# Larger query packets, a shorter prologue list and a reordered first batch in a retention and MLP kernel

## The chip, the cores and the metric

The kernel runs on one core of a Trainium2 chip. Its engines are TensorE (matmuls, "PE" in the profile; its weight loads are "PEld"), VectorE ("DVE"), ScalarE ("ACT"), GpSimd ("POOL") and SyncE ("SP"), which here only issues DMAs. The metric is device time in microseconds (us), and a kernel's time is the median of its runs. A change counts as faster or slower when its ratio to the kernel before is clear of 1 by more than 2%; a 95% interval stands beside each ratio.

## The reference

There are two stages. The first is a retention layer: attention without softmax, in which each score is weighted by a power of a decay per head. The second mixes tokens through a low-rank pair U, V, adds, and applies an MLP.

```python
# q, k, v: (8 batches, 8 heads, 576 tokens, 64), fp32
scores = (q @ k.T) / sqrt(64)
D[i, j] = gamma[h] ** (i - j) if i >= j else 0
ret = (scores * D) @ v                     # per batch and head
x = ret, heads put side by side            # (8, 576, 512)
u = x + ((x.T @ U) @ V).T                  # U: (576, 32), V: (32, 576)
out = u + relu(u @ w1) @ w2                # w1: (512, 2048), w2: (2048, 512)
```

## The kernel before

Batches are taken in pairs. The 1152 tokens of a pair make nine chunks of 128 rows; chunk XC = 4, the joint chunk, holds the last 64 tokens of the even batch and the first 64 of the odd one. The decay is split into a factor for q and a factor for k and v, so that each chunk needs one triangular mask (`ret`), and a running state k^T v per batch (`ps_s`, copied to `s_sb`) carries the past chunks. The MLP works on nine groups of four chunks of 128 tokens. Its first layer is called Y1 below and its second Y2. TensorE has about 320 us of work, and attention of later batches is woven in between the matmuls of the MLP.

A planner in the kernel simulates the engines and writes down a fixed order of instructions for each. Every engine then runs its list strictly in that order. An instruction that waits holds up everything behind it on its engine, and any edit lets the planner find another order elsewhere.

The loads, and what becomes of them, are the part that the change touches. In the kernel before, each chunk loads q and k as a pair into one staging buffer, and a row of the transfer is one head of one token: 64 values of 4 bytes, or 256 B.

```python
N = dict(kq=5, vs=6, qkv=8, qkT=6, ret=6, s_sb=3, ...)          # buffers of each kind
kqs = [sbuf(f"kq_{i}_st", [P, 2, H, D], FP32) for i in range(N["kq"])]
...
for n, (j, dram) in enumerate(((1, k), (0, q), (2, v))):        # in load(p, c, ...)
    ...
    nc.sync.dma_start(out=f[rw, :, :],
        in_=dram[b, :, t0:t0 + rw.stop - rw.start, :].rearrange("h s d -> s h d"))
...
if early:                                                       # the first pair
    ck = pl.op("ACT", 660.0, lambda e: cast(e, 1, 2), [got[1]], ...)      # k, to bf16
    cq = pl.op("DVE", 700.0, qsc, [got[0], ck, cons], ...)                # q times its factor
    cv = pl.op("POOL", 1050.0, vsc, ..., alt=[("DVE", 700.0)])            # v times its factor
else:                                                           # the other pairs
    ck = cq = pl.op("DVE", 700.0, lambda e: cast(e, 0, 2), [got[1], got[0]], ...)  # k and q
```

V is loaded four times, into four groups of 32 partitions. The loads of the first pair are issued in one fixed line: q and k of the first batch, three of its v, U, the rest of v, V, the weights, then the second batch.

```python
for i in range(4):
    nc.sync.dma_start(out=vst[i * R:(i + 1) * R, :], in_=moe_V)
...
first = [0, 1, XC, 2, 3]
line = [ld[x, (0, c)] for c in first for x in "kq"] + [ld["v", (0, c)] for c in (0, 1, 2)]
line += [ld["lu"], ld["v", (0, XC)], ld["v", (0, 3)], ld["lv"]] + ld["lw"]
line += [ld[x, (0, c)] for c in range(5, NCH) for x in "kq"]
line += [ld["v", (0, c)] for c in range(5, NCH)]
```

## Time and profile before

The median was 346.05 us of three runs (346.04 to 346.5). These are lines of the profile's page.

```profile
span 346.1 us, 5817 instructions
...
PE 323.8 (94%) x2348; PEld 158.8 (46%) x2348; DVE 142.4 (41%) x206; ACT 136.6 (39%) x237; POOL 72.7 (21%) x97
...
PE   2679989999998899999999999999999999999995
...
DMA  9979999999999999999999999951211131011002
GB/s 165 210 155 357 385 273 246 225 239 196 186 221 198 221 203 182 238 200 213 196 193 212 204 206 207 216 138 31 82 59 29 30 91 61 2 61 61 2 36 85
...
PE 71%; DMA 14%; SPq 6%; DVE 4%; issue 1%; ACT 1%; POOL 0%; DVEq 0%; POOLq 0%
```

The second line gives busy time and share of the span for each engine. The next rows cut the span into 40 slices of 8.65 us: busy tenths of TensorE and of the DMA engines, and what the DMAs moved. The last line shares out the chain of work that ended last. TensorE is 94% busy, and short of it at three places: the first three slices, the sixth (43 to 52 us), and the 13th and 14th (104 to 121 us). The DMA row is full up to about 225 us. It moves only some 200 GB/s where q, k and v arrive and 385 GB/s where the weights do (fifth slice).

The view by windows gives sizes to these. The columns are the window, its length, and busy time with number of instructions for TensorE, its weight loads, DVE, ACT and POOL; then the clock, the DMA share and GB/s.

```profile
0.00:30.00 30.00, 18.79 (x189) 11.65 (x189) 14.06 (x35) 15.02 (x28) 7.38 (x19) 1.00 0.99 195
50.00:80.00 30.00, 27.12 (x262) 14.70 (x261) 18.52 (x28) 15.72 (x29) 9.28 (x11) 1.00 1.01 224
100.00:130.00 30.00, 26.86 (x212) 12.89 (x210) 14.43 (x19) 9.03 (x16) 7.18 (x9) 1.00 1.07 212
```

I also use a second measure, "gaps": the time from one matmul's start to the next one's, less 0.213 us for 512 columns and in proportion for fewer (the spacing seen in full stretches is 0.216 us), counted where it exceeds 15 ns. By it the kernel before loses 17.9 us from 0 to 30 us, 6.4 from 50 to 80 and 4.8 from 100 to 130.

Three marks on TensorE's timeline: the first MLP matmul at 31.60 us ("MLP 0"), the first of the second group at 75.69 ("MLP 1"), and the end.

### The profile page before, as it was taken

To read this page: it belongs to the slowest core of one execution; us is meant where nothing else is said; L and a number is where in the kernel's file an instruction comes from. 1 tells how busy PE (TensorE), PEld (TensorE's weight loads), DVE (VectorE), ACT (ScalarE), POOL (GpSimd) and SP (SyncE) were. 2 spreads that over 40 slices of the span, in tenths; PEclk is the share of its full clock that TensorE was granted. 3 is DMA by queue.
4 is the path that set the end of the run, shared out by engine and by line. 5 is a ranking of instruction groups with operands and counts; after the bars stand their busy time and mean duration, and the time that the engine had idled before them with its cause. 6 is when DMAs were issued, how large, how long until landed. Compare 5 with 4: busy or idle time off the path is not lost.

```text
span 346.1 us, 5817 instructions
## 1 busy us (share of the span) xinstructions
PE 323.8 (94%) x2348; PEld 158.8 (46%) x2348; DVE 142.4 (41%) x206; ACT 136.6 (39%) x237; POOL 72.7 (21%) x97
## 2 busy tenths in 40 slices
PE   2679989999998899999999999999999999999995
PEld 1354434545543444454445445544544444444442
DVE  2743106657645452565527436734453020021011
ACT  5535636458720354035512641255115405503600
POOL 1046671232231221312213112310110010011010
PEclk9999999999999999999999999999999999999999
DMA  9979999999999999999999999951211131011002
GB/s 165 210 155 357 385 273 246 225 239 196 186 221 198 221 203 182 238 200 213 196 193 212 204 206 207 216 138 31 82 59 29 30 91 61 2 61 61 2 36 85
DMA packets 159769, 56.39 MB, mean 163 GB/s; under 512 B 153088, under 2 KB 153088, under 8 KB 159744
## 3 DMA queue, kind: packets, MB, share of 16 engines
q1 hardware_dynamic: 157024, 47.12, 70.6%
q0 software_dynamic: 2720, 8.92, 8.0%
q8 instruction: 18, 0.29, 0.4%
q14 instruction: 7, 0.06, 0.1%
HBM read 37.14 MB, written 9.44 MB: 135 GB/s over the span
## 4 chain that ended last, share of the span: by engine, by line
PE 71%; DMA 14%; SPq 6%; DVE 4%; issue 1%; ACT 1%; POOL 0%; DVEq 0%; POOLq 0%
PE ps_big_t L263 61%; DMA kq_st<-in_q_dram 9%; SPq L297 5%; PE ps_o L263 4%; PE ps_s L263 4%; DMA kq_st<-in_k_dram 2%; PE ps_sc L263 2%; DMA v_st<-in_v_dram 2%; DMA ust<-in_moe_U_dram 1%; DVE ret_t L438 1%; DVE qkv_t L318 1%; SPq L578 1%; DVE u_t L566 1%; DVE o_sb L672 1%; DVE qkv_t L322 1%
## 5 line engine op out<-in xcount | busy, mean ns | idle before, releaser
L263 PE MATMUL ps_big_t<-uT_t,w_sb 128*128 128x512 bf16 x576 | 134.0, 379 | 1.0 <-DMA uT_t<-u_t 1.0
L263 PE MATMUL ps_big_t<-w_sb,y_t 128*128 128x512 bf16 x576 | 133.0, 379 | 0.0
L648 ACT ACTIVATE y_t<-ps_big_t 128x512 bf16<-128x512 f32 x144 | 86.0, 597 | 99.1 <-PE ps_big_t L263 98.9
L263 PEld LDWEIGHTS <-w_sb 128*128 128x128 bf16 x576 | 53.8, 98 | 63.8 <-issue 3.4
L263 PEld LDWEIGHTS <-y_t 128*128 128x128 bf16 x576 | 54.0, 98 | 63.1 <-issue 2.9
L672 DVE TENSOR_TENSOR o_sb<-ps_big_t,u_t 128x512 f32<-128x512 f32 x36 | 24.8, 688 | 86.1 <-PE ps_big_t L263 84.4
L322 POOL TENSOR_TENSOR qkv_t<-v_st,vscale 128x512 bf16<-128x512 f32 x32 | 33.5, 1047 | 98.1 <-DMA v_st<-in_v_dram 61.4
L678 POOL DMA_DIRECT2D out_dram<-o_sb x34 | 19.2, 564 | 153.4 <-DVE o_sb L672 153.4
L438 DVE TENSOR_TENSOR ret_t<-ps_sc,tri 128x1024 bf16<-128x1024 f32 (+1 forms) x36 | 39.2, 1099 | 19.6 <-PE ps_sc L263 19.6
L406 ACT ACTIVATE s_sb<-ps_s 128x512 bf16<-128x512 f32 x32 | 19.1, 596 | 64.0 <-PE ps_s L263 64.0
L318 DVE CAST qkv_t<-kq_st 128x1024 bf16<-128x1024 f32 x27 | 20.6, 764 | 27.9 <-DMA kq_st<-in_q_dram 27.9
L502 DVE TENSOR_TENSOR x_t<-ps_o,qscale 128x512 bf16<-128x512 f32 x27 | 18.6, 687 | 13.9 <-PE ps_o L263 13.8
L369 PE MATMUL ps_big_t<-ident,qkv_t 128*128 128x128 bf16 x112 | 12.4, 251 | 10.9 <-ACT qkv_t L316 9.0
L566 DVE TENSOR_TENSOR u_t<-ps_s,x_t 128x512 bf16<-128x512 f32 x20 | 13.7, 687 | 16.5 <-PE ps_s L263 16.5
L263 PEld LDWEIGHTS <-qkT_t 64*128 64x128 bf16 (+1 forms) x544 | 14.6, 98 | 12.2 <-issue 7.9
L376 ACT ACTIVATE qkT_t<-ps_big_t 128x512 bf16<-128x512 bf16 x28 | 16.4, 594 | 6.6 <-PE ps_big_t L369 6.1
L263 PEld LDWEIGHTS <-ret_t 128*128 128x128 bf16 x288 | 13.6, 102 | 9.0 <-DVE ret_t L438 1.6
L263 PE MATMUL ps_sc<-qkT_t 64*128 64x128 bf16 x288 | 15.4, 230 | 1.0 <-DVE ret_t L438 0.8
L263 PE MATMUL ps_o<-qkv_t,ret_t 128*128 128x64 bf16 x288 | 15.3, 199 | 0.8 <-DVE ret_t L438 0.6
L322 DVE TENSOR_TENSOR qkv_t<-kq_st,qscale 128x512 bf16<-128x512 f32 x9 | 6.2, 690 | 22.6 <-DMA kq_st<-in_q_dram 22.6
L369 PEld LDWEIGHTS <-qkv_t 128*128 128x128 bf16 x112 | 7.9, 109 | 15.6 <-ACT qkv_t L316 10.6
L263 PE MATMUL ps_s<-qkv_t 128*128 128x128 bf16 (+1 forms) x128 | 13.3, 230 | 1.0 <-POOL qkv_t L322 0.5
(58 smaller groups left out, 121.8 us busy)
## 6 DMA issues: line engine op xcount, KB each, us to landing
out_dram<-o_sb POOLq DMA_DIRECT2D x34, 256.0 KB, 3.1
kq_st<-in_k_dram SPq DMA_DIRECT2D x32, 256.0 KB, 4.9
kq_st<-in_q_dram SPq DMA_DIRECT2D x32, 256.0 KB, 5.1
v_st<-in_v_dram SPq DMA_DIRECT2D x32, 256.0 KB, 5.2
y_t<-in_moe_w_ch_dram SPq DMA_DIRECT2D x10, 512.0 KB, 8.5
wst_t<-in_moe_w_ch_dram SPq DMA_DIRECT2D x6, 512.0 KB, 6.9
kq_st<-in_k_dram SPq DMA_DIRECT2D x8, 128.0 KB, 4.1
kq_st<-in_q_dram SPq DMA_DIRECT2D x8, 128.0 KB, 4.4
```

The source lines that it names most:

```text
L263: nc.tensor.matmul(*a, skip_group_check=True, **kw)
L297: i = nc.sync.dma_start(out=f[rw, :, :], in_=dram[b, :, t0:t0 + rw.stop - rw.start, :].rearrange("h s d -> s h d"),)
L318: nc.vector.tensor_copy(**args)
L322: eng.tensor_tensor(out=qkv[slot(*qk)][:, j, :, :], in0=f, in1=by[:, c, :, None].to_broadcast([P, H, D]), op=ALU.mult,)
L369: nc.tensor.transpose(pst()[:, hp, :], t[:, j, 2 * hp:2 * hp + 2, :].rearrange("p h d -> p (h d)"), ident,)
L406: nc.scalar.activation(out=s_sb[slot(*sk)], in_=ps_s.rearrange("p (a b) -> p a b", b=P), func=AF.Copy)
L438: nc.vector.tensor_tensor(out=ret[slot(*rk)][:, s], in0=ps_sc[:, s], in1=m[:, None, None, :].to_broadcast([P, n, NHP, P]), op=ALU.mult,)
L502: nc.vector.tensor_tensor(out=xs[slot(*xk)].rearrange("p hp hl d -> p hl hp d"), in0=ps_o[:, :, 0:NHP * D].rearrange("p hl (hp d) -> p hl ...
L566: nc.vector.tensor_tensor(out=us[slot(*uk)].rearrange("p (hp hl d) -> p hp hl d", hl=2, d=D), in0=bank().rearrange("p (hp hl d) -> p hp hl ...
L648: nc.scalar.activation(out=y1s[slot(*yk)][:, f, :], in_=ps_big[slot(*bk)], func=AF.Relu)
L672: nc.vector.tensor_tensor(out=osb[slot(*ok)], in0=ps_big[slot(*bk)], in1=us[slot(*uk)], op=ALU.add)
L678: eng.dma_start(out=out_flat[row:row + P, :], in_=osb[slot(*ok)])
```

## The change

The intent is to shorten the stretch before TensorE is full. It has six parts.

1. The q of batches 0 and 1 comes in one 1 MB DMA each. A partition takes four neighbouring tokens, so a row is 1 KB. The rows are then in the wrong order; the four PSUM evacuations of q^T put it right.
2. The joint chunk is computed in 64x64 blocks instead of whole.
3. Chunks 1 and 3 of the first batch put their scores into two other PSUM buffers, so that they need not wait for the mask of the chunk before.
4. V is loaded once and copied three times on GpSimd; U's second half is loaded after the weights.
5. k, q and v have separate staging buffers (12, and 4 for q), and k and q are cast apart.
6. The planner may look 150 ns ahead on DVE and ACT, and the first batch runs in the order 0, 1, 2, 3, XC.

```diff
+    LOOK = {"DVE": 150.0, "ACT": 150.0}
-    N = dict(kq=5, vs=6, qkv=8, qkT=6, ret=6, s_sb=3, x=7, u=12, wst=6, osb=3)
+    N = dict(st=12, q4s=4, qkv=8, qkT=6, ret=6, s_sb=3, x=7, u=12, wst=6, osb=3)
 ...
+    def load_q4(par, prio):
+            nc.sync.dma_start(
+                out=q4.rearrange("p (h x) -> p h x", h=H),
+                in_=q[par, :, t0:t0 + 4 * P, :].rearrange("h (p r) d -> p h (r d)", r=4))
 ...
+            st["q", c] = pl.op("DVE", 700.0, ..., alt=[("POOL", 1050.0)])      # q times its factor
+    def t_q4(par, prio):
+        pst = ps_sc.bitcast(BF16).rearrange("p a b n -> p (a b n)").rearrange(
+            "p (r hp l) -> p r hp l", r=4, hp=NHP)                             # two PSUM banks
+        for i in range(4):
+                args = dict(
+                    out=qkT[slot("qkT", (0, c))][:, 0:NHP, :].rearrange("p hp (l r) -> p hp l r", r=4),
+                    in_=pst[:, :, :, 32 * i:32 * i + 32].rearrange("p r hp l -> p hp l r"))
+            st["qT", c] = pl.op("ACT", 600.0, ev, pes, ..., rel=[sck], alt=[("DVE", 650.0)])
 ...
-            ck = cq = pl.op("DVE", 700.0, lambda e: cast(e, 0, 2), [got[1], got[0]], prio + 4, [qk])
+            ck = pl.op("DVE", 370.0, lambda e: cast(e, 1), [got[1]], prio + 4, [qk])
+            st["q", c] = pl.op("DVE", 370.0, lambda e: cast(e, 0), [got[0], ck], prio + 4, rel=[home[0]])
 ...
-            for i in range(4):
-                nc.sync.dma_start(out=vst[i * R:(i + 1) * R, :], in_=moe_V)
+            nc.sync.dma_start(out=vst, in_=moe_V)
+            for i in range(1, 4):
+                gp.tensor_copy(out=VV[i * R:(i + 1) * R, 0:S], in_=VV[0:R, 0:S])
 ...
-        for n, c in enumerate((0, 1, XC, 2, 3)):
+        for n, c in enumerate((0, 1, 2, 3, XC)):
-            SC(0, c, pr + 3, with_q=False, split=True)
+            SC(0, c, pr + 3, with_q=False, apart=c in (1, 3))
 ...
-    line = [ld[x, (0, c)] for c in first for x in "kq"] + [ld["v", (0, c)] for c in (0, 1, 2)]
-    line += [ld["lu"], ld["v", (0, XC)], ld["v", (0, 3)], ld["lv"]] + ld["lw"]
-    line += [ld[x, (0, c)] for c in range(5, NCH) for x in "kq"]
+    line = [ld["q4", 0]] + [ld["k", (0, c)] for c in first] + [ld["q", (0, XC)]]
+    line += [ld["lv"], ld["lu"]] + [ld["v", (0, c)] for c in first] + ld["lw"]
+    line += [ld["q4", 1]] + [ld["k", (0, c)] for c in range(5, NCH)] + [ld["lub"]]
```

## The prediction

> **What bounds the kernel now.** By the page's busy row, TensorE: 323.8 of 346.1 us at full clock (0.999). From the first MLP matmul at 31.6 us (timeline) it is nearly full, and no work is taken from it. Lost are (a) the 31.6 us before, with about 18 us of TensorE gaps, (b) about 6.4 us of gaps from 50 to 80 us (second batch's attention under the first MLP group; the largest, 2.0 us at 50.5, waits for that batch's first keys), (c) about 5 us from 100 to 130 us, (d) a 4 us tail. (a) and (b) are DMA-bound: the page's DMA row stands at 9 tenths from 0 to 210 us, and the chain of waits names loads of q, k, v and U before these gaps.
>
> **What the change does.** q, k, v come in 256-byte packets, 1024 for each 256 KB, a load every 1.2 to 1.3 us (10 to 16 us: 5065 packets, 213 GB/s). Weights in 2 KB packets take 87 ns each against 18 to 25 ns for 256 B: 389 GB/s. This agrees with the Trainium skill, "DMA: Bandwidth & Descriptors", Specifications, which puts line rate at transfers of at least 512 B. My estimate from these for 1 KB rows is 45 ns a packet, so 1 MB of q takes 2.8 us in place of about 5: 2.3 us saved in each of batches 0 and 1. U's second half (576 packets of 128 B) moves behind the weights: 0.5 us. V once instead of four times: 0.6 us of bytes; and 5 small issues of 0.4 to 0.6 us leave SyncE's queue between 16 and 23.5 us, where DMA ran at only 149 to 174 GB/s and the first weights landed 4.5 us after the last v (29.1, 24.6).
>
> Added: three VV copies (0.6 to 0.7 us), k casts (1.0) and q scalings (1.05) on GpSimd, in all about 13 us before the weight casts, which fits into its waits for DMA. q's reordering rides on the four PSUM evacuations (0.6 us each). Two score buffers take the mask (1.28 us) off the matmul path, but the prologue waits for DMA, so that is worth little. The joint chunk in 64x64 blocks saves about 0.6 us of DVE in each of four chunks, off the critical path; separate k and q casts cost DVE a little.
>
> **Sum.** The first batch's last v lands near 21 us (24.6), the first MLP matmul comes near 26.5 (31.6): 5 us, all critical. The weights' end moves from 46.5 to about 42. The second batch needs 1 MB of q before its first transposes, so its first stall stays (about 2 us), but its last v comes 1.5 to 2 us sooner still; second MLP group near 67.5 against 75.7: 8 us, of which I give 1 back (one Y2 group moves before it). The later gaps stay, because loads and TensorE move together.
>
> **Prediction: 338.7 us**, 8 in 10 between 334.5 and 343.0. Faster by over 2% (below 339.1): 0.55; within 2%: 0.42; slower: 0.03.
>
> **What would show it.** 1 KB packets near 45 ns; last first-batch v near 21 us; first MLP group from 25.5 to 28 us, second from 66 to 70; TensorE gaps of 4 to 6 us between 45 and 75; TensorE's busy time unchanged within 2 us; from the second MLP group to the end about 270 us, as before.
>
> **What would make it wrong.** GpSimd's longer list delays v's scaling or the first weight casts; 1 KB packets no faster per byte; the 1 MB load delays all transposes; the planner's new look-ahead reorders ACT and DVE so that later gaps grow; four q staging buffers (five before) slow the later prefetch. Upwards: the gaps from 100 to 130 us shrink too.

## More of the kernel before

Between 100 and 130 us TensorE lacks 3.1 us. Two more views say why. First the waits of DVE from 70 to 140 us (us in total, times, longest):

```profile
DVE qkv_t L318 <- DMA kq_st<-in_q_dram: 22.4, 11, 5.1
```

Then DVE's timeline there (start, length, and in brackets the idle time before it and what ended it):

```profile
104.29 0.69 DVE L318 CAST qkv_t<-kq_st 128x1024 bf16<-128x1024 f32 x1 [2.81 <-DMA kq_st<-in_q_dram]
104.90 0.68 DVE L566 TENSOR_TENSOR u_t<-ps_s,x_t 128x512 bf16<-128x512 f32 x1
...
122.86 0.69 DVE L318 CAST qkv_t<-kq_st 128x1024 bf16<-128x1024 f32 x1 [2.67 <-DMA kq_st<-in_q_dram]
123.46 0.68 DVE L502 TENSOR_TENSOR x_t<-ps_o,qscale 128x512 bf16<-128x512 f32 x1
```

And TensorE's:

```profile
105.63 0.38 PE L263 MATMUL ps_s<-a_sb,VV 128*128 128x512 bf16 x1 [1.28 <-DVE u_t L566]
...
116.47 1.89 PE L263 MATMUL ps_big_t<-uT_t,w_sb 128*128 128x512 bf16 x8 [1.04 <-DMA uT_t<-u_t]
...
124.20 0.29 PE L263 MATMUL ps_o<-s_sb,qkT_t 64*128 64x64 bf16 x8 [0.82 <-DVE x_t L502]
```

A cast of q and k waits on DVE for its load. The results that TensorE needs, `u_t` and `x_t`, stand behind it in DVE's list, and TensorE waits for those.

In the first batch the view by tile gives the same picture: DVE waits for all five q loads (6.3 us) and ACT for all five k loads (4.4 us). Busy time hides some of what TensorE loses, because a matmul of 128 columns counts 0.31 us in the first 22 us and 0.22 us after 30 us.

## The result

The changed kernel took 341.66 us (340.43 to 341.9, four runs), against 346.27 us (346.04 to 347.2, four runs) for the kernel before in the same rounds. The ratio is 0.9855, with a 95% interval of 0.9824 to 0.9885: faster by 1.45%, which is within 2%. Ratios here and below are the mean time of one kernel's fast runs over that of the other's of the same rounds, so they are not quite the ratio of the medians quoted.

The time lies inside the predicted range, 3 us above its middle. A gain of over 2%, to which the prediction gave 0.55, did not come. The terms of the sum did worse, and that is the subject of the rest.

The page of the changed kernel:

```profile
span 339.8 us, 5955 instructions
...
PE 320.3 (94%) x2412; PEld 159.2 (47%) x2412; DVE 156.1 (46%) x227; ACT 132.8 (39%) x234; POOL 86.0 (25%) x116
...
GB/s 212 202 292 390 385 249 262 213 258 211 206 236 197 229 183 223 210 219 207 183 238 224 195 216 202 125 15 44 66 64 15 69 87 31 0 64 62 0 64 63
...
PE 89%; DVE 5%; DMA 2%; issue 1%; ACT 1%; POOL 0%; DVEq 0%; POOLq 0%
```

DMA had 14% of the chain that ended last, and now has 2%; TensorE's share of it rose from 71% to 89%. The weights' rate is reached one slice sooner. The same windows as before:

```profile
0.00:30.00 30.00, 18.10 (x211) 12.55 (x212) 14.31 (x30) 13.46 (x27) 20.70 (x38) 1.00 1.09 258
50.00:80.00 30.00, 27.66 (x290) 16.08 (x290) 25.06 (x35) 15.55 (x30) 10.84 (x14) 1.00 1.09 237
100.00:130.00 30.00, 30.00 (x235) 14.51 (x234) 18.78 (x25) 12.40 (x21) 6.89 (x8) 1.00 1.07 210
```

From 0 to 30 us TensorE is no busier than before, although the DMAs moved a third more (258 GB/s against 195). From 100 to 130 us it is full. The same stages side by side:

| | before | after | predicted |
|---|---|---|---|
| first weight load issued, us | 23.5 | 17.7 | - |
| MLP 0, us | 31.60 | 30.09 | 26.5 (25.5 to 28) |
| MLP 1, us | 75.69 | 72.39 | 67.5 (66 to 70) |
| from MLP 1 to the end, us | 270.4 | 267.4 | about 270 |
| gaps, 50 to 80 us | 6.4 | 4.9 | 4 to 6 from 45 to 75 |
| gaps, 100 to 130 us | 4.8 | 1.2 | "stay" |
| TensorE busy, us | 323.8 | 320.3 | within 2 of before |

The spans differ by 6.3 us and the medians by 4.6. The profiled execution of the kernel before was a slow one for it, 347.9 us on the timer against a median of 346.27; that of the changed kernel was 341.9 against 341.66. Single stages can therefore be off by a microsecond or so. One such place shows: at 50.5 us the kernel before loses 2.0 us to its wait for the second batch's first k, and b_fastq1 (below), which loads the same things up to 60.7 us, loses 0.6 there. So some 1.4 of the 3.3 us at MLP 1 may be the slow execution's. A repeat of the changed kernel, told of below, had MLP 0 at 29.31 us.

### The prologue: loads sooner, first state matmul not

The first batch on DVE, before:

```profile
8.23 0.69 DVE L322 TENSOR_TENSOR qkv_t<-kq_st,qscale 128x512 bf16<-128x512 f32 x1 [2.33 <-DMA kq_st<-in_q_dram]
8.84 1.28 DVE L438 TENSOR_TENSOR ret_t<-ps_sc,tri 128x512 bf16<-128x512 f32 x2
...
24.66 0.69 DVE L322 TENSOR_TENSOR qkv_t<-v_st,vscale 128x512 bf16<-128x512 f32 x1 [2.67 <-DMA v_st<-in_v_dram]
```

And in the changed kernel:

```profile
6.57 2.14 DVE L307 TENSOR_TENSOR qkv_t<-q_st,qs 128x512 bf16<-128x512 f32 x2 [3.74 <-DMA q_st<-in_q_dram]
10.31 0.69 DVE L359 COPY qkT_t<-ps_sc 128x512 bf16<-128x512 bf16 x1 [1.60 <-PE ps_sc L343]
11.67 0.69 DVE L359 COPY qkT_t<-ps_sc 128x512 bf16<-128x512 bf16 x1 [0.66 <-ACT qkT_t L357]
14.29 1.23 DVE L533 TENSOR_TENSOR ret_t<-ps_sc,tri 128x1024 bf16<-128x1024 f32 x1 [1.93 <-PE ps_sc L278]
...
17.75 1.09 DVE L307 TENSOR_TENSOR qkv_t<-st_st,vscale 128x512 bf16<-128x512 f32 x1
```

ACT does the other two of the four evacuations:

```profile
11.04 0.60 ACT L357 ACTIVATE qkT_t<-ps_sc 128x512 bf16<-128x512 bf16 x1 [1.51 <-DVE qkT_t L359]
12.39 0.60 ACT L357 ACTIVATE qkT_t<-ps_sc 128x512 bf16<-128x512 bf16 x1 [0.76 <-DVE qkT_t L359]
```

GpSimd has a list it did not have before (before, it did nothing on this batch until 17.22 us, when the first v landed):

```profile
6.62 2.99 POOL L307 TENSOR_TENSOR qkv_t<-q_st,qs 128x512 bf16<-128x512 f32 x2 [2.47 <-DMA q_st<-in_q_dram]
...
16.24 2.06 POOL L816 COPY VV<-VV 32x576 bf16<-32x576 bf16 x3
18.39 2.36 POOL L307 TENSOR_TENSOR qkv_t<-st_st,vscale 128x512 bf16<-128x512 f32 x2
```

Here is what to see. In the kernel before the first q is on DVE at 5.21 us, the chunks follow each other as their loads land, and the first mask starts at 8.84. In the changed kernel nothing starts before the whole megabyte has landed at 6.5 us; two scalings each on DVE and GpSimd take until 9.6; the four evacuations run strictly in turn, DVE, ACT, DVE, ACT, from 10.31 to 12.99; the first mask starts at 14.29. Then DVE is at masks until 17.8 us without a pause, and GpSimd has V to copy. So the first v, which no longer waits for DMA (no bracket at 17.75 and 18.39), is scaled at 17.75 us against 17.22. It landed at 16.17 us, 0.9 us sooner than before (17.08), and then lay for 1.6 us. The first state matmul, k^T v, needs it, and starts at 18.90 us against 18.60.

From there to MLP 0 comes a serial run: for each chunk a state matmul, its evacuation, the output matmul, its evacuation, a transpose and the product with U. It took 13.0 us before, with waits for v and U in it, and 11.2 us in the change, with no wait for a load. All of the prologue's gain is here.

The missing waits need not be the whole cause of it; I had overlooked TensorE's clock. The same product with U is slow at first and then fast, here in the changed kernel:

```profile
21.82 0.61 PE L278 MATMUL ps_big_t<-x_t,UU 128*32 128x512 bf16 x1
...
24.81 0.39 PE L278 MATMUL ps_big_t<-x_t,UU 128*32 128x512 bf16 x1
```

The trace's first record of a full clock is at 24.73 us. Until then matmuls of 128 columns follow each other every 107 ns, later every 56. In the kernel before, that record is at 28.16 us, and the product still takes 0.61 us at 27.43. (The page prints a clock of 1.00 also where it has no record; in a_onebuf the stretch from 14.0 to 24.3 us is recorded, as 0.5.) Over all 14 traces the run from the first state matmul to MLP 0 is 0.48 us longer for each microsecond of it that lies before the full clock (correlation 0.98). From before to after that part shrank from 9.6 to 5.8 us, which by this line is 1.8 us, as much as the run shrank. So the clock is a rival to the waits as the cause of this gain. No run separates them, and none shows what brings the full clock on.

### From 100 to 130 us: the wait that went away

DVE's waits for loads from 70 to 140 us were 22.4 us before. In the changed kernel the same view has one line of that kind:

```profile
DVE qkv_t L403 <- DMA q_st<-in_q_dram: 0.9, 1, 0.9
```

The loads of the second pair (batches 2 and 3) start at 52.6 us, against 62.6. The tenth chunk after the first pair, which is the first of the third pair, has its k load issued at 91.7 us, against 105.8. MLP 1 moved by 3.3 us in the same time. The view of waits lists none for TensorE between 100 and 130 us.

### The profile page after: what moved, and what is told of

Same layout as the page of the kernel before. It is cut to its first block, busy times and chain, and to the rows that moved or that the text cites. A ratio compares the mean times of both kernels' runs of the same rounds, so it can differ in the third digit from the quotient of the medians.

```text
span 339.8 us, 5955 instructions
## 1 busy us (share of the span) xinstructions
PE 320.3 (94%) x2412; PEld 159.2 (47%) x2412; DVE 156.1 (46%) x227; ACT 132.8 (39%) x234; POOL 86.0 (25%) x116
## 4 chain that ended last, share of the span: by engine, by line
PE 89%; DVE 5%; DMA 2%; issue 1%; ACT 1%; POOL 0%; DVEq 0%; POOLq 0%
PE ps_big_t L278 73%; PE ps_o L278 6%; PE ps_s L278 5%; PE ps_sc L278 4%; DMA q_st<-in_q_dram 2%; DVE ret_t L533 2%; DVE qkv_t L307 1%; PE ps_big_t L452 1%; PE ps_sc L343 1%; DVE qkv_t L403 1%; ACT qkT_t L357 1%; DVE qkT_t L359 1%; POOL qkv_t L307 0%; DVE o_sb L776 0%; DVE u_t L670 0%
## 5 line engine op out<-in xcount | busy, mean ns | idle before, releaser
L776 DVE TENSOR_TENSOR o_sb<-ps_big_t,u_t 128x512 f32<-128x512 f32 x36 | 24.8, 689 | 90.4 <-PE ps_big_t L278 88.1
L307 POOL TENSOR_TENSOR qkv_t<-st_st,vscale 128x512 bf16<-128x512 f32 x32 | 33.9, 1063 | 52.0 <-DMA st_st<-in_v_dram 26.1
L533 DVE TENSOR_TENSOR ret_t<-ps_sc,tri 128x1024 bf16<-128x1024 f32 x30 | 36.6, 1219 | 18.4 <-PE ps_sc L278 18.4
L403 DVE CAST qkv_t<-st_st 128x512 bf16<-128x512 f32 x27 | 21.5, 795 | 0.8 <-DMA st_st<-in_k_dram 0.8
L278 PEld LDWEIGHTS <-qkT_t 64*128 64x128 bf16 (+2 forms) x576 | 15.0, 100 | 13.4 <-issue 7.1
L278 PEld LDWEIGHTS <-ret_t 128*128 128x128 bf16 (+1 forms) x320 | 13.3, 103 | 9.2 <-DVE ret_t L533 1.6
L278 PE MATMUL ps_sc<-qkT_t 64*128 64x128 bf16 (+1 forms) x304 | 13.7, 221 | 4.0 <-ACT qkT_t L459 2.1
L278 PE MATMUL ps_o<-qkv_t,ret_t 128*128 128x64 bf16 (+1 forms) x320 | 15.2, 197 | 0.9 <-DVE x_t L600 0.5
L403 DVE CAST qkv_t<-q_st 128x512 bf16<-128x512 f32 x27 | 14.3, 529 | 1.4 <-DMA q_st<-in_q_dram 1.4
L278 PEld LDWEIGHTS <-qkv_t 128*128 128x128 bf16 (+1 forms) x128 | 9.2, 102 | 6.1 <-issue 2.1
L670 DVE TENSOR_TENSOR u_t<-ps_o,x_t 128x512 bf16<-128x512 f32 x16 | 10.9, 684 | 1.7 <-PE ps_o L278 1.6
```

Source lines behind the costliest of these rows:

```text
L278: nc.tensor.matmul(*a, skip_group_check=True, **kw)
L307: eng.tensor_tensor(out=out, in0=f, in1=by[:, :, None].to_broadcast([P, H, D]), op=ALU.mult)
L403: nc.vector.tensor_copy(**args)
L533: nc.vector.tensor_tensor(out=ret[slot(*rk)][:, hl, :, 0:n], in0=bank(hl.start)[:, None] if apart else ps_sc[:, hl, :, 0:n], in1=m[:, None ...
L670: nc.vector.tensor_tensor(out=us[slot(*uk)].rearrange("p (hp hl d) -> p hp hl d", hl=2, d=D), in0=bank().rearrange("p (hp hl d) -> p hp hl ...
L776: nc.vector.tensor_tensor(out=osb[slot(*ok)], in0=ps_big[slot(*bk)], in1=us[slot(*uk)], op=ALU.add)
```

## The experiments

Twelve runs followed. The names say what each starts from: "a" from the changed kernel, "b" from the kernel before. Each was timed in three to five rounds beside the kernel before, which had medians of 346.21, 347.35 and 346.74 us, and each has one profile. For all runs:

| run | median, us | ratio to before, 95% | MLP 0 | first state matmul | gaps 100 to 130 |
|---|---|---|---|---|---|
| the change | 341.66 | 0.9855 [0.9824, 0.9885] | 30.09 | 18.90 | 1.2 |
| a_again, the change once more | 341.79 | 0.9849 [0.9806, 0.9892] | 29.31 | 18.19 | 2.0* |
| a_banksplit | 341.0 | 0.9849 [0.9809, 0.9889] | 28.96 | 17.24 | 1.2 |
| a_fastv0, wrong | 341.05 | 0.985 [0.9827, 0.9874] | 29.68 | 18.51 | 1.2 |
| a_q256 | 343.62 | 0.9922 [0.9889, 0.9955] | 31.69 | 18.22 | 1.3 |
| a_onebuf | 343.18 | 0.9871 [0.9829, 0.9913] | 30.06 | 18.07 | 2.0* |
| a_nolook | 340.8 | 0.9799 [0.9752, 0.9845] | 29.19 | 18.89 | 2.1* |
| a_xcwhole | 344.42 | 0.9912 [0.9845, 0.998] | 28.49 | 18.32 | 2.0* |
| a_best | 341.12 | 0.9829 [0.9791, 0.9868] | 29.74 | 19.48 | 2.3* |
| b_fastq1, wrong | 343.24 | 0.9909 [0.9881, 0.9937] | 31.44 | 18.49 | 1.3 |
| b_uv | 345.94 | 0.996 [0.9912, 1.0007] | 32.48 | 18.18 | 5.1* |
| b_split | 345.96 | 0.9974 [0.9922, 1.0026] | 30.35 | 18.10 | 4.2* |
| b_uvsplit | 347.03 | 0.9999 [0.995, 1.0047] | 32.20 | 18.27 | 4.7* |

The traces marked * lack some forty matmul records more than the others, and each missing record looks like a gap of 0.22 us or more. By the stretches where nothing waits, that adds about 0.8 us to 30 us, so 2.0 there is about 1.2, and 4.2 about 3.4.

Two questions were put. Why did the prologue give 1.5 us instead of 5? And why did the gaps from 100 to 130 us close, which I had said would stay?

### a_banksplit: evacuations of different banks

Theory: the four evacuations run in turn because all four read both PSUM banks, and this delays the masks and all after them. The edit lays q^T out so that each bank holds two of the four head pairs, and splits each evacuation by bank: ACT reads one, DVE the other. Buffers are taken at the transposes, and the planner counts free buffers when one operation takes two of a pool.

```diff
-            "p (r hp l) -> p r hp l", r=4, hp=NHP)
+            "p (hp r l) -> p r hp l", r=4, hp=NHP)
...
+            for half in range(2):
+                hs = slice(2 * half, 2 * half + 2)
...
+                        out=qkT[slot("qkT", (0, c))][:, hs, :].rearrange("p hp (l r) -> p hp l r", r=4),
+                        in_=pst[:, :, hs, 32 * i:32 * i + 32].rearrange("p r hp l -> p hp l r"))
...
+                st["qT", c].append(pl.op(("ACT", "DVE")[half], 400.0, ev, pes, ..., rel=[sck]))
```

> The change, but q^T leaves PSUM in halves by bank (two head pairs each): ScalarE from one bank, VectorE from the other, at the same time, where the change has the two engines take turns (10.3 to 13.0 us). Theory 'the prologue is a chain of compute': the four copies end near 12 us, the first MLP group starts about 1 us sooner (29.0 to 29.4 us against 30.1), total 0.5 to 1 us below the change. Rival 'the prologue is still bound by DMA': first MLP group unchanged at 30.1, total unchanged.

The evacuations did run side by side. This is DVE's timeline:

```profile
10.13 1.42 DVE L364 COPY qkT_t<-ps_sc 128x256 bf16<-128x256 bf16 x4 [1.60 <-PE ps_sc L343]
12.64 1.22 DVE L539 TENSOR_TENSOR ret_t<-ps_sc,tri 128x1024 bf16<-128x1024 f32 x1 [1.09 <-PE ps_sc L278]
```

They end at 11.55 us instead of 12.99, and the first mask starts 1.65 us sooner. The first state matmul came 1.66 us sooner, at 17.24 (against the repeat of the change, told of below, 1.34 for the mask and 0.95 for the matmul). But the run from there to MLP 0 grew from 11.2 to 11.7 us, and the median fell by 0.7 us, which the intervals don't separate from nothing. So the order of the evacuations is a real cost, but the next limit lies close behind it: the last v had to wait for its load there (0.95 us on GpSimd at 22.56), and the first one had landed at 15.95 us, only 0.16 us before DVE scaled it.

### a_fastv0: is it still the DMA?

The rival says that the prologue still waits for DMA. In this run the first batch's v comes in 2 KB rows of contiguous memory. The values are wrong (relative error 0.52), but every other step is the same.

```diff
+                    if j == 2 and p == 0 and c <= XC:
+                        n = (rw.stop - rw.start) * H * D
+                        a0 = t0 * H * D
+                        sent.append(nc.sync.dma_start(
+                            out=f[rw, :, :].rearrange("p h d -> p (h d)"),
+                            in_=dram[b].rearrange("h s d -> (h s d)")[a0:a0 + n].rearrange("(p x) -> p x", x=H * D),
+                        ))
+                        continue
```

> The change, but the first batch's v (and the joint chunk's) come in 2 KB rows of the same bytes, so with wrong data on purpose: about 4 us less DMA in the prologue. Theory 'chain of compute': first MLP group within 0.5 us of 30.1. Rival 'still bound by DMA': it starts 2 to 4 us sooner. Total: within 1.5 us of the change by the theory, 3 us or more below it by the rival.

The last v was issued at 14.97 us instead of 17.06, and the first weight at 15.6 instead of 17.7: 2.1 us less of DMA, where I had expected 4. The first v landed at 15.61 us instead of 16.17, and DVE scaled it at 17.78, no sooner than in the change (17.75). MLP 0 came at 29.68 us, between the 30.09 and 29.31 of the change's own two traces. The ratio, 0.985, is the change's. The rival falls: two microseconds less of DMA in the prologue buy nothing that can be told from the scatter.

### a_q256: without the 1 KB rows

The q of the first pair is loaded chunk by chunk in 256 B rows again; all else is the change.

```diff
-        wide = p == 0 and c != XC
+        wide = False
...
-        load_q4(0, base - 3.0)
-        t_q4(0, base - 2.0)
...
-    line = [ld["q4", 0]] + [ld["k", (0, c)] for c in first] + [ld["q", (0, XC)]]
+    line = [ld[x, (0, c)] for c in first for x in "kq"]
```

> The change, but q of the first two batches in 256-byte rows again, chunk by chunk, transposed as in the kernel before; V once, staging, casts, look-ahead, two score buffers and 64x64 blocks kept. Theory 'the 1 KB rows pay through the lead of the loads': first MLP group within 1.5 us of 30.1, but the later loads 4 to 5 us later, so second MLP group 74 to 76 us, TensorE gaps from 100 to 130 us back to 2 to 4 us (1.2 with the change), total 343 to 346. Rival 'the order of instructions or VectorE's lighter load closed the gaps': gaps from 100 to 130 stay under 1.5 us.

It took 343.62 us, ratio 0.9922 against 0.9855, so the 1 KB rows with all that hangs on them are worth about 0.7%. The trace shows that this isn't the prologue alone. MLP 0 is at 31.69 us, 1.6 later, but MLP 1 is at 72.20, no later than the change's 72.39, because gaps from 50 to 80 us are 2.7 us in place of 4.9. The change's second batch also waits for a whole megabyte of q and four evacuations in turn. Nor did the gaps from 100 to 130 us come back to 2 to 4 us, as my theory of the 1 KB rows had it: at 1.3 us they kept to what its rival said. What is lost is one stall that the change doesn't have:

```profile
151.17 0.41 PE L278 MATMUL ps_o<-qkv_t,ret_t 128*128 128x64 bf16 x8 [2.67 <-DVE ret_t L533]
```

Behind it DVE waited 1.59 and 1.68 us for two loads, issued at 143.5 us and later, after a DMA transpose had held SyncE's list from 140.7 to 143.5. Whether every run of this kernel has this stall is not known; I have one trace of it.

### b_fastq1: only the loads of the second pair, on the kernel before

Theory: the gaps from 100 to 130 us are waits for loads of the second pair. In this run only that pair's q is loaded in 2 KB rows of contiguous memory (wrong values again, relative error 0.67). Nothing else differs from the kernel before.

```diff
+                    if j == 0 and p == 1:
+                        ...                     # the same 2 KB rows as in a_fastv0, for q
+                        continue
```

> The kernel before, but q of the second pair of batches in 2 KB rows of as many bytes, so with wrong data on purpose: less DMA after 62 us, nothing else touched. Theory 'gaps from 100 to 130 us are VectorE's queue standing behind casts that wait for q': first and second MLP group unchanged (31.6, 75.7), VectorE's waits for q between 70 and 140 us fall from 22 us to under 8, TensorE gaps from 100 to 130 fall from 4.8 us to under 2, total 342 to 344. Rival 'order and VectorE load': gaps stay at 4 us or more, total 346.

Gaps from 100 to 130 us fell from 4.8 to 1.3 us, and DVE's waits for loads from 22.4 to 12.9 us (I had expected under 8). The time fell to 343.24 us, ratio 0.9909. MLP 0 stayed where it was (31.44). This shows that the gaps were load waits. Relief for the loads of the second pair is worth about 0.9% by itself, more than half of what the whole change gained. MLP 1 came 2.2 us sooner, at 73.47, and gaps from 50 to 80 us fell from 6.4 to 4.3 us, which I had not expected; but 1.4 us of that is at 50.5 us, before the first of the changed loads was issued, so the edit did not cause it. From MLP 1 to the end the trace is 3.3 us shorter.

### b_uv: V once and U's second half later, on the kernel before

What in the change closes those gaps? My first theory was that any relief of the DMA early on is enough, since the DMAs are full up to about 225 us. This run has part 4 of the change alone.

```diff
-            for i in range(4):
-                nc.sync.dma_start(out=vst[i * R:(i + 1) * R, :], in_=moe_V)
+            nc.sync.dma_start(out=vst, in_=moe_V)
...
+            for i in range(1, 4):
+                gp.tensor_copy(out=VV[i * R:(i + 1) * R, 0:S], in_=VV[0:R, 0:S])
...
-    line += [ld["lu"], ld["v", (0, XC)], ld["v", (0, 3)], ld["lv"]] + ld["lw"]
-    line += [ld[x, (0, c)] for c in range(5, NCH) for x in "kq"]
+    line += [ld["lv"], ld["lu"], ld["v", (0, XC)], ld["v", (0, 3)]] + ld["lw"]
+    line += [ld[x, (0, c)] for c in range(5, NCH) for x in "kq"] + [ld["lub"]]
```

> The kernel before with one part of the change alone: V loaded once and copied on GpSimd, U's second half behind the second batch's keys. Theory 'a small relief of DMA and of SyncE's queue gives most of the lead': the first weight load is issued near 20.5 us (23.5 before, 17.7 with the change), the first MLP group starts at 30 to 31 us (31.6), TensorE gaps from 100 to 130 us fall from 4.8 to under 2.5, total 342 to 344. Rival 'the 1 KB rows are needed for it': gaps from 100 to 130 stay at 4 us or more and the total at 345 to 346.

The weights were issued 4.1 us sooner (19.4), yet MLP 0 came 0.9 us later, at 32.48: the casts and copies of V and U take GpSimd from 20.3 to 24.4 us, DVE scales the v's at 22.98 and 24.16 us, the first of them after 2.82 us of waiting for its load, and TensorE waits 1.64 us at 24.30 for a result that stands behind it on DVE. DVE's waits barely changed:

```profile
DVE qkv_t L318 <- DMA kq_st<-in_q_dram: 21.0, 10, 5.4
```

The gaps stayed (5.1), and the time is 345.94 us, ratio 0.996 with an interval that holds 1. The theory falls. MLP 1 came 2.6 us sooner and the k load of the tenth chunk after the first pair 2.7 us sooner: here loads and TensorE moved together, as the prediction had said.

### a_onebuf: one score buffer in the first batch

```diff
-            SC(0, c, pr + 3, with_q=False, apart=c in (1, 3))
+            SC(0, c, pr + 3, with_q=False, apart=False)
```

> The change, but all score blocks of the first batch in the one buffer, masks whole, as elsewhere. Theory 'the prologue is a chain of compute': first MLP group 0.5 to 1.5 us later than 30.1, total up by as much. Rival, as I predicted ('worth little, the prologue waits for DMA'): within 0.3 us.

MLP 0 is at 30.06 us, which is the change's 30.09. The median is 343.18 us, 1.4 to 1.5 above the change's, but the ratio (0.9871 against 0.9855) is not separated from it. The first state matmul came no later. The second buffers are worth little in the prologue, as predicted.

### a_nolook: the planner without its look-ahead

```diff
-    LOOK = {"DVE": 150.0, "ACT": 150.0}
+    LOOK = {}
```

> The change without the planner's look-ahead on VectorE and ScalarE, so another order of a few instructions. Theory 'the gain is the lead of the loads': total within 1 us of the change, gaps from 100 to 130 us under 2. Rival 'the new order closed the gaps': they come back to 4 us, total 344 or more.

It took 340.8 us, ratio 0.9799: nothing is lost without the look-ahead, and nominally 0.9 us is gained (1.9 us by the ratios, as the kernel before was slower). The gaps from 100 to 130 us stay closed. This run also gives a measure of luck. It computes the same things in another order, and differs from the change by 1 to 2 us. No part that is worth less than that can be told from the planner's rearrangement.

### a_xcwhole: the joint chunk whole

```diff
-        n = HALF if c == XC else P
+        n = P
...
+        cols = slice(0, HALF) if c == XC else slice(0, P)
```

> The change, but the joint chunk whole again (128x128 scores, block mask, full state copy). VectorE's mask for it takes 1.2 us again in place of 0.69 in each of four chunks. Theory: off the critical path, total within 0.7 us of the change, gaps from 100 to 130 us under 2. Rival 'VectorE's lighter load closed the gaps': they come back to 3 us or more, total 343 or more.

It took 344.42 us (342.28 to 347.4), ratio 0.9912 with the wide interval 0.9845 to 0.998. That is nominally 0.6% worse than the change, although MLP 0 came at 28.49 us, the earliest of all. The trace is that of the slowest run, with a stall of 2.4 us at 147.6 us, and a clock recorded at 0.5 from 151.4 to 158.2 us; no other trace has such a stretch after 30 us and before its end. The mean granted clock doesn't order the runs: the fastest had 0.983, and two of 344.4 us had 0.998 and 1.0. The blocks may be worth up to 2 us, or the order may have been unlucky. This stays open.

### b_split: separate staging and casts, on the kernel before

My second theory for the gaps: the joint cast of k and q waits for both loads at the head of DVE's list, and the change casts them apart, from buffers that are freed one by one. This run has part 5 alone, with 16 staging buffers.

```diff
-    N = dict(kq=5, vs=6, qkv=8, qkT=6, ret=6, s_sb=3, x=7, u=12, wst=6, osb=3)
+    N = dict(st=16, qkv=8, qkT=6, ret=6, s_sb=3, x=7, u=12, wst=6, osb=3)
...
-            ck = cq = pl.op("DVE", 700.0, lambda e: cast(e, 0, 2), [got[1], got[0]], prio + 4, [qk])
+            ck = pl.op("DVE", 370.0, lambda e: cast(e, 1), [got[1]], prio + 4, [qk])
+            cq = pl.op("DVE", 370.0, lambda e: cast(e, 0), [got[0], ck], prio + 4)
```

> The kernel before with another part of the change alone: one staging buffer for each load (16) in place of 5 pairs and 6, and k and q cast apart on VectorE; loads, V and all else as before. Theory 'a cast that waits for both loads of a pair holds up VectorE's queue': first and second MLP group unchanged (31.6, 75.7), VectorE's waits for loads between 70 and 140 us fall from 22 us to under 12, TensorE gaps from 100 to 130 us from 4.8 to under 2.5, total 342 to 344. Rival 'it takes less DMA': gaps stay at 4 us or more, total 345.5 to 347.

The gaps stayed for the most part (4.2, or about 3.4 with the missing records allowed for), and DVE waited 17.8 us for loads. The time is 345.96 us, ratio 0.9974. The second theory falls as well.

### b_uvsplit: both parts together

The edit is that of b_uv and that of b_split, in one kernel.

> The kernel before with both: V once and U's second half later, and one staging buffer for each load with k and q cast apart; q still in 256-byte rows. Theory 'neither alone, both together': total 342.5 to 344.5, gaps from 100 to 130 us under 2.5, near the change with q in 256-byte rows (343.6). Theory 'the 1 KB rows are needed': 345 or more, gaps at 4 us or more.

The time is 347.03 us, ratio 0.9999, with gaps of 4.7 us. Parts 4 and 5 together don't close the gaps.

### a_again: the change once more

No edit; it is a measure of the scatter, in five rounds.

> The changed kernel once more, unchanged, as the measure for the next run on the same chip: 341 to 342.5 us.

It took 341.79 us (341.48 to 341.87). Its MLP 0 was at 29.31 us, 0.8 us before that of the first trace, and 0.7 of that was there at the first state matmul already. Single marks of one trace are good to about 0.8 us; the medians agree within 0.15 us.

### a_best: a version meant to beat both

This joins what the runs suggested: evacuations split by bank as in a_banksplit, q scaled on DVE alone, and v on GpSimd alone.

```diff
+            ...                                  # evacuations and buffer count as in a_banksplit
-                [got, ld["consts"]], prio + 0.1, acq=[("qkv", (0, c))], rel=[keys[r]],
-                alt=[("POOL", 1050.0)])
+                [got, ld["consts"]], prio + 0.1, acq=[("qkv", (0, c))], rel=[keys[r]])
...
-            cv = pl.op("POOL", 1050.0, vsc, [got[2], ck, cons], prio + 1.2, alt=[("DVE", 700.0)])
-            if c == NCH - 1:
-                cv.engs = [("DVE", 700.0)]
+            cv = pl.op("POOL", 1050.0, vsc, [got[2], ck, cons], prio + 1.2)
```

> The change, with q^T's halves leaving PSUM at the same time by bank, and in the first two batches q scaled on VectorE alone and v on GpSimd alone, so that neither stands behind the other[...] (1.53 us in place of 0.69 for VectorE, 1.54 in place of 1.04 for GpSimd). Theory 'the prologue is a chain of compute with those two waits in it': first MLP group 28.3 to 29.3 us (30.1), gaps from 50 to 80 us under 4 (4.9), total 1 to 2.5 us below the change. Rival: first MLP group as with the banks alone (29.0), total within 0.7 us of the change.

DVE's timeline shows that the first half of the plan worked:

```profile
6.40 2.50 DVE L307 TENSOR_TENSOR qkv_t<-q_st,qs 128x512 bf16<-128x512 f32 x4 [3.58 <-DMA q_st<-in_q_dram]
9.68 1.42 DVE L363 COPY qkT_t<-ps_sc 128x256 bf16<-128x256 bf16 x4 [0.78 <-PE ps_sc L342]
12.18 1.23 DVE L536 TENSOR_TENSOR ret_t<-ps_sc,tri 128x1024 bf16<-128x1024 f32 x1 [1.09 <-PE ps_sc L278]
```

GpSimd's shows where the gain went:

```profile
16.24 2.06 POOL L819 COPY VV<-VV 32x576 bf16<-32x576 bf16 x3
18.39 5.07 POOL L307 TENSOR_TENSOR qkv_t<-st_st,vscale 128x512 bf16<-128x512 f32 x5
```

Four scalings on DVE without GpSimd beside it take 2.50 us for all; shared between both engines they took until 9.6 us. The first mask starts 2.1 us sooner than in the change. But now every v stands behind the V copies on GpSimd, the first state matmul comes at 19.48 us, and MLP 0 at 29.74. The run took 341.12 us against 341.79 of the change in the same rounds; the means, 341.11 and 341.73, differ by 0.6 us or 0.2%. It is the better kernel by a hair, and it missed the gain that I expected of it: the total is the rival's.

## Why the prediction was right or wrong

**"What bounds the kernel now": partly wrong.** The prologue was DMA-bound before, and DVE's and ACT's waits for q and k show it. But it was also one step away from being bound by its own chain of computation, and that decided the outcome. The dip from 100 to 130 us was noted as (c) and left without a cause; the DVE lines at 104.29 and 122.86 would have named it.

**Packets of 1 KB "near 45 ns": right.** The median of the 1 KB packets was 46 ns, against 18 to 29 for 256 B and 84 to 88 for 2 KB. This agrees with the Trainium skill, "DMA: Bandwidth & Descriptors", Specifications, which gives 512 B as the least transfer for line rate. My estimate from the uncrowded values (18, 46 and 84 ns) is some 8 ns for each packet and 38 ns for each KB; 16 engines would then move 227, 356 and 390 GB/s.

**"The first batch's last v lands near 21 us (24.6)": right.** The last of it was issued at 17.06 us and took 4.1 us to land: 21.2. The first weight load was issued at 17.7 us in place of 23.5, and its first cast began at 23.20 in place of 29.12.

**"The first MLP matmul comes near 26.5 (31.6): 5 us, all critical": wrong, and this is the first step that failed.** It came at 30.09 us, and at 29.31 in the repeat. I let MLP 0 follow the last v. What it follows is the first state matmul, plus a serial run of 10.2 to 12.0 us in the changed kernel and its variants (13.5 in a_q256, whose q comes late), and the length of that run goes with the time at which TensorE's clock becomes full (above). That first matmul needs the first v, scaled. The first v's load was issued at 12.31 us against 12.02 before, since V and half of U had moved ahead of it, and it landed at 16.17 against 17.08. But when it had landed, DVE was busy with masks until 17.8 us and GpSimd with q, k and V until 18.4. a_fastv0 shows that DMA no longer limits this stretch, and a_banksplit shows that the evacuations in turn are one part of what does: without them the first state matmul came 1.66 us sooner than in the change's first trace and 0.95 sooner than in its second. a_best shows the next part by its trace, the V copies before v on GpSimd. "GpSimd's longer list delays v's scaling" was on my list of what would make the prediction wrong. Only a_banksplit had both an early mask and a first v that DVE scaled as soon as it landed. My estimate for what more could be had is its first state matmul and the shortest run to MLP 0 (10.2 us, in a_xcwhole, whose clock was full 3.4 us after the first state matmul): 17.2 + 10.2 = 27.4 us. It is untested, and it takes for granted that the last v is there in time and that the clock is full as soon.

That the evacuations run in turn has a reason in the kernel's ordering of readers of one PSUM bank. The Trainium skill, "PSUM — Partial Sum Buffer", section "PSUM bank collisions raise a hardware error", says that any two engines on one bank and the same 32 partitions collide, reads by ScalarE and VectorE included, and that software has to keep them apart. The trace agrees as far as it can: readers of both banks took turns (2.68 us for four), and readers of one bank each ran together (1.42 us).

**"q's reordering rides on the four PSUM evacuations (0.6 us each)": the size was right, the place was not.** They took 0.60 to 0.69 us each, but in turn on the critical path. The same is true of "q scalings (1.05) on GpSimd": they took 1.54 and 1.49 us, and DVE's second scaling beside them 1.53 us in place of 0.69. This agrees with the Trainium skill, "SBUF — State Buffer", section "Who interferes with whom": a DVE instruction with two SBUF inputs contends with a GpSimd instruction that reads SBUF.

**"Its first stall stays (about 2 us)", and gaps of 4 to 6 us from 45 to 75: right in size (4.8 us).** The largest wait there is 1.46 us at 54.66, for an evacuation of the second batch's q^T, so for computation and not for the megabyte of q that I had named. "Second MLP group near 67.5" was wrong by 4.9 us, of which 3.6 are the first batch's: from MLP 0 to MLP 1 the change took 42.3 us, against 44.1 before and 41.0 predicted.

**"The later gaps stay, because loads and TensorE move together": wrong, and this is the second step that failed.** They closed: 4.8 to 1.2 us. b_fastq1 shows that they were waits for loads. The later loads did not move with TensorE but gained on it. The time from MLP 1 to the issue of the k load of the tenth chunk after the first pair sorts all the traces:

| trace | k load of the tenth chunk, us | less MLP 1, us | gaps 100 to 130 |
|---|---|---|---|
| before | 105.8 | 30.1 | 4.8 |
| b_uv | 103.2 | 30.1 | 5.1* |
| b_split | 102.8 | 29.0 | 4.2* |
| b_uvsplit | 101.2 | 28.3 | 4.7* |
| b_fastq1 | 100.0 | 26.5 | 1.3 |
| a_q256 | 97.7 | 25.5 | 1.3 |
| a_onebuf | 96.3 | 24.8 | 2.0* |
| a_xcwhole | 97.7 | 25.4 | 2.0* |
| a_nolook | 95.9 | 24.5 | 2.1* |
| a_banksplit | 95.8 | 23.0 | 1.2 |
| a_best | 95.2 | 22.6 | 2.3* |
| a_fastv0 | 93.6 | 21.6 | 1.2 |
| a_again | 91.9 | 20.0 | 2.0* |
| after | 91.7 | 19.3 | 1.2 |

At 28 us or more the gaps are open, at 26.5 or less they are closed. My reading, argued from this table and not tested on its own, is that it counts whether the loads get a lead of a few microseconds over the place where DVE meets them. Which parts of the change make the lead is not settled. Taking away the 1 KB rows, the second score buffers, the look-ahead or the blocks, one at a time, leaves the gaps closed; parts 4 and 5 of the change, on the kernel before, don't close them, neither alone nor together. It takes a combination that I didn't find.

**"Two score buffers ... worth little": right** for MLP 0. **"The joint chunk ... off the critical path": not settled** (a_xcwhole). **"The planner's new look-ahead reorders ACT and DVE so that later gaps grow": did not happen,** and a_nolook shows no gain from it either. **"Four q staging buffers slow the later prefetch": did not happen;** the prefetch ran sooner.

**"Separate casts cost DVE a little": too small.** The group of k casts averaged 795 ns and that of q casts 529, together 35.8 us, against 20.6 us for the joint casts before. Part of them were held:

```profile
103.15 1.69 DVE L403 CAST qkv_t<-st_st 128x512 bf16<-128x512 f32 x1
104.76 0.41 DVE L403 CAST qkv_t<-q_st 128x512 bf16<-128x512 f32 x1
```

The two casts have the same size. While the first ran, GpSimd scaled a v from 103.49 us for 1.05 us. DVE had the room, and TensorE did not wait for it there.

**"TensorE's busy time unchanged within 2 us": missed,** at 3.5 us less (323.8 to 320.3). Of this, 1.9 us is before MLP 0, where the full clock came 3.4 us sooner; the rest is not explained.

**The sum: right for a wrong reason.** I expected 8 us by MLP 1 and got 3.3 (1.9, if the 1.4 us at 50.5 us are the slow execution's); I expected none after it, apart from the 1 us I gave back, and got 3.0. The errors, 4.7 us short and 4.0 us over in these spans, nearly cancel. That the median is still 3 us above my number is for the larger part the slow profiled execution of the kernel before, 1.6 us over its median, from which I took the spans. Of the 4.6 us by the medians, b_fastq1 says that relief of the second pair's loads can account for about 3 (0.0091 of 346 us); that the prologue and the second batch make the rest is an inference, since the parts weren't shown to add up.

## What to carry to other kernels

When a prologue is bound by loads, write down the chain of computation that will be left once the loads are faster, with the engine that each step will find busy, and count the gain only up to it; a landing time is not a start time. Look there at the time per column of the matmuls too, before a gain is put down to waits. Where an engine runs its list in order, look for loads awaited at the head of that list far from the place being tuned: a lead of a few microseconds there can be worth more than the stretch that the change was made for. And where every edit lets a planner rearrange the rest, run the change twice and one variant that alters only the order, so that the size of a difference that means nothing is known before parts are given credit.

## What the Trainium skill lacked or had wrong

- "DMA: Bandwidth & Descriptors" gives 512 B as the least transfer for line rate, but its measured table is for DMAs issued from GpSimd, by size of the whole transfer, and for the cost of small packets it has a share of bus cycles but no time per packet for trn2 loads issued by SyncE. The runs show 18 to 29 ns for 256 B, 46 ns for 1 KB and 84 to 88 ns for 2 KB, at some 160 to 240 GB/s where rows were 256 B and 380 to 390 GB/s where they were 2 KB.
- "SBUF — State Buffer", "Who interferes with whom", is borne out, but gives no sizes for these instructions. The runs show a DVE scaling of 128x512 at 0.69 us alone and 1.53 us beside GpSimd, GpSimd's own at 1.04 and 1.54 us, and a DVE cast of 128x512 at 0.41 us alone and 1.69 us held.
- The same section says that whoever issues first keeps the shared ports. The records show a cast that starts at 103.15 us, 0.34 us before GpSimd's instruction, and still ends 0.3 us after it (again at 111.48). "Perfetto Trace Analysis", section "GPSIMD Engine Instruction", warns that GpSimd's recorded span is unreliable, so its true start may have been earlier; and in both places GpSimd was issuing a DMA just before (102.94 to 103.48 and 111.27 to 111.81 us). No run here settles it.
- "PSUM — Partial Sum Buffer" says that readers of one bank have to be kept apart, but not what that costs. Four evacuations of both banks took 2.68 us in turn; laid out so that each engine had a bank of its own, the same work took 1.42 us.
